# Weights and stores on GpSimd's queue, sixteen transposes by DMA, and a new instruction order in a hand-scheduled kernel

**Chip, cores, metric.** One core of one Trainium2 chip. The metric is device time in microseconds (us) of one execution.

## The reference

A decaying-state attention over 4 batches, 8 heads, 768 steps and head size 48, then a two-layer MLP with SoLU and layer norm (3072 tokens, 384 to 1024 to 384):

```python
for t in range(S):
    cur = np.einsum('bhd,bhe->bhde', u[None] * kt, vt)
    y[:, :, t] = np.einsum('bhd,bhde->bhe', rt, state + cur)
    state = wt[:, :, :, None] * state + np.einsum('bhd,bhe->bhde', kt, vt)
...
h = x @ w_in                       # x is y, rearranged to tokens x 384
e = np.exp(h - h_max); sm = e / e.sum()
solu = h * sm
ln = (solu - mean) / sqrt(var + 1e-6) * g_ln
out = ln @ w_out
```

## The kernel before

The kernel cuts time into 6 chunks of 128 steps; with 4 batches that makes 24 *units*. The whole program is one string of words. Each word is one stage of one unit, its number is the unit, and the letter behind the point is an engine, a queue or a PSUM slot. Every engine and every DMA queue carries out its words **in the order of the string**.

```python
ORDER = """
LW0.a LK0.s LU0.a LR0.s LW1.a LW2.s hot4.s3 LG0.s LK1.s lw0 LV0.a cum0.b0 LR1.s us0.s0 ex0 hot2.s3 uc0 lw1 LV1.s
p0 kp0 LW3.a LK2.a LR2.s krk0.s3 q0 krr0 cum1.b1 kr0.a hot2.s2 LV2.s ...
...                                              # 57 rows left out
o23.a out23
"""
```

The words that matter here: `LW LK LR LV` load a unit's w, k, r, v and `LI LO` the MLP's weights; `lw cum ex kp` make the scaled k and r; `krk krr kr` turn them on TensorE (PE) and copy them out of PSUM, `KD` does the same with one DMA; `y` is the attention's result, `X xT` turn it on PE and copy it, `XD` does that by DMA; `H e he hq` are the hidden layer, its exponential, their product and its square; `Oa Ob ... o out` are the output matmuls, the scaling and the store; `ce` centres the second weight matrix.

```python
    queue = {"s": sp, "a": act}
    ...
    def turned_kr(i, x):                                   # KD
        sp.dma_start_transpose(out=kr_s[i % NKP], in_=kp_t[i % NKP].rearrange("t j h d -> t (j h d)"))

    def turned_x(i, x):                                    # XD
        sp.dma_start_transpose(out=xT_t[i % NWK], in_=y_t[i % NWK])

    def hidden_mul(i, x):                                  # he: one input in PSUM
        dve.tensor_mul(out=he_t[i % NWK], in0=live[i]["h_ps"], in1=e_t[i % NWK])

    def hidden_square(i, x):                               # hq: both inputs in SBUF
        he, hq = he_t[i % NWK], hq_t[i % NWK]
        if x == "a":
            act.activation(out=hq, in_=he, func=SQUARE)
        else:
            (dve if x == "d" else pool).tensor_mul(out=hq, in0=he, in1=he)

    def store(i, x):
        c, b = units[i]
        sp.dma_start(out=out[b * S + c * C:b * S + (c + 1) * C, :], in_=o_t[i % NWK])
```

The softmax here doesn't subtract the row's maximum and nothing guards it: scores larger than these inputs give would overflow.

## Time and profile before

| | before |
|---|---|
| median of 4 runs (range) | 152.42 us (151.28 to 153.02) |
| span of the profiled run, mean granted PE clock | 151.6 us, 0.994 |
| start of the first / last o_ps matmul | 33.7 / 146.8 us |
| from there to the end | 4.8 us |

The first and the last matmul into o_ps are good milestones: before the first one the kernel loads, after the last one it only scales and stores. (The prediction had three of the four runs, with a median of 152.2.) First, the row of VectorE's (DVE's) squares in the table of instruction groups (busy us, mean ns, idle us before):

```profile
L89 DVE TENSOR_TENSOR hq<-he 128x1024 bf16<-128x1024 bf16 x11 | 8.2, 757 | 0.0
```

The median of the eleven is 681 ns, so the mean hides a longer one. The timeline (start us, length us) shows it between GpSimd's (POOL's) instructions:

```profile
86.78 1.00 POOL L89 TENSOR_TENSOR p<-kr_in 128x384 bf16<-128x384 f32 x1
87.73 1.55 POOL L89 TENSOR_SCALAR_AFFINE_SELECT m<-m 128x1024 bf16<-128x1024 bf16 x1
...
86.91 1.42 DVE L89 TENSOR_TENSOR hq<-he 128x1024 bf16<-128x1024 bf16 x1
```

The square begins while GpSimd's `p` runs and ends 0.55 us after `p` has ended, and the mask that follows takes 1.55 us in place of its usual 1.1. So it reads as if the two engines took turns: the square's real 0.68 us begins about where `p` ends, and the mask waits for it.

### The profile page before, as it was taken

Reading aid. Unit: us, or ns where it says so; the run is one execution under the profiler, and the core shown is the slowest. Engines: PE = TensorE matmul, PEld = TensorE weight load, DVE = VectorE, ACT = ScalarE, POOL = GpSimd, SP = SyncE. Lnnn points to the kernel's source line nnn. Section 1 sums busy time; section 2 is a strip of 40 time slices with the busy share of each in tenths; the row PEclk is TensorE's granted clock in tenths of the full one; section 3 lists DMA queues with packets and bytes.
Section 4 is the critical chain, followed back from the end, with each engine's and each line's share of the span. In section 5 each row is a group of like instructions: output and inputs, shape, how many; then the busy total and the mean of one; then the engine's idle time right before and its main releaser. Section 6 shows DMA issues by size and latency. Waiting matters only on the chain.

```text
span 151.6 us, 5258 instructions
## 1 busy us (share of the span) xinstructions
PE 137.2 (91%) x2156; PEld 106.6 (70%) x2158; DVE 127.9 (84%) x235; ACT 117.9 (78%) x238; POOL 94.9 (63%) x127
## 2 busy tenths in 40 slices
PE   4799787879999997999988999999999999999980
PEld 1145566467788776888777797878887888889650
DVE  5209797999999996999976999999998998688940
ACT  3465766599999997999798688999898997484442
POOL 7484993531879859993849999299847682500000
PEclk9999999999999999999999999999999999999997
DMA  5999999999983999989699999898950111011142
GB/s 110 259 257 334 405 335 255 178 210 188 224 179 121 229 217 193 215 176 241 142 243 208 230 175 232 162 230 193 248 164 6 52 56 52 4 52 56 52 160 104
DMA packets 104825, 27.08 MB, mean 179 GB/s; under 512 B 100313, under 2 KB 104418, under 8 KB 104802
## 3 DMA queue, kind: packets, MB, share of 16 engines
q1 hardware_dynamic: 94256, 24.26, 69.6%
q10 hardware_dynamic: 10546, 2.49, 7.3%
q8 instruction: 17, 0.28, 0.7%
q14 instruction: 6, 0.05, 0.1%
HBM read 22.03 MB, written 4.72 MB: 176 GB/s over the span
## 4 chain that ended last, share of the span: by engine, by line
PE 54%; DMA 12%; SPq 10%; DVE 8%; ACT 6%; POOL 4%; issue 4%; ACTq 0%; POOLq 0%
PE o_ps L89 22%; PE h_ps L89 13%; SPq L89 10%; DMA w_in<-in_w_dram 6%; PE kr_ps L89 4%; PE y_ps L89 4%; DMA kr_in<-in_r_dram 4%; PE s_ps L89 3%; PE cum_ps L89 3%; PE m_ps L89 3%; DMA v_in<-in_v_dram 3%; PE x_ps L89 2%; DVE he L89 1%; POOL m L89 1%; DVE w L89 1%
## 5 line engine op out<-in xcount | busy, mean ns | idle before, releaser
L89 PE MATMUL o_ps<-w,he 128*128 128x385 bf16 x192 | 45.7, 325 | 0.1
L89 PE MATMUL h_ps<-xT,win_sb 128*128 128x128 bf16 x576 | 35.9, 219 | 0.3 <-DVE xT L89 0.3
L89 PEld LDWEIGHTS <-win_sb 128*128 128x128 bf16 x576 | 33.0, 98 | 0.9 <-issue 0.4
L89 PE MATMUL o_ps<-inv_col,e 128*128 128x1 bf16 x192 | 31.7, 165 | 0.0
L89 DVE TENSOR_TENSOR he<-h_ps,e 128x1024 bf16<-128x1024 f32 x24 | 29.1, 1216 | 2.7 <-ACT e L89 2.5
L89 PE MATMUL o_ps<-one_col,hq 128*128 128x1 bf16 x192 | 31.3, 163 | 0.0
L89 ACT ACTIVATE e<-h_ps 128x1024 bf16<-128x1024 f32 x24 | 24.5, 1020 | 4.7 <-PE h_ps L89 4.6
L89 DVE TENSOR_TENSOR kp<-cum_ps,kr_in 128x768 bf16<-128x768 f32 x24 | 22.7, 948 | 5.9 <-ACT cum_ps L89 5.6
L89 PEld LDWEIGHTS <-hq 128*128 128x128 bf16 x192 | 18.5, 96 | 12.8
L89 POOL TENSOR_TENSOR p<-kr_in 128x384 bf16<-128x384 f32 x24 | 24.4, 1018 | 3.7 <-DMA kr_in<-in_r_dram 3.6
L89 POOL TENSOR_TENSOR dv<-vb,dg 128x384 bf16<-128x384 bf16 x24 | 19.8, 830 | 9.6 <-DVE dg L89 7.4
L89 POOL TENSOR_SCALAR_AFFINE_SELECT m<-m 128x1024 bf16<-128x1024 bf16 x15 | 16.8, 1120 | 13.4 <-ACT sq L89 5.8
L89 POOL TENSOR_TENSOR q<-p,u_bc 128x384 bf16<-128x384 bf16 x24 | 21.8, 911 | 1.9 <-ACT u_bc L89 1.7
L89 PEld LDWEIGHTS <-kp 128*128 128x128 bf16 x272 | 17.4, 98 | 6.0 <-DVE kp L89 2.1
L89 ACT ACTIVATE cum_ps<-cum_ps 128x768 f32<-128x768 f32 x24 | 19.2, 802 | 3.0 <-PE cum_ps L89 2.9
L89 PE MATMUL kr_ps<-ident,kp 128*128 128x128 bf16 x192 | 18.0, 222 | 2.3 <-ACT gr L89 0.8
L89 PEld LDWEIGHTS <-he 128*128 128x128 bf16 x192 | 18.4, 96 | 0.9
L89 PEld LDWEIGHTS <-e 128*128 128x128 bf16 x192 | 18.4, 96 | 0.5 <-issue 0.2
L89 ACT ACTIVATE lw<-w_in 128x384 bf16<-128x384 f32 x24 | 12.4, 523 | 4.1 <-DMA w_in<-in_w_dram 4.1
L89 ACT CAST m<-m_ps 128x1024 bf16<-128x1024 f32 x15 | 15.0, 1013 | 0.7 <-PE m_ps L89 0.6
L89 DVE TENSOR_TENSOR m<-m_ps,keep 128x1024 bf16<-128x1024 f32 x9 | 10.9, 1215 | 4.2 <-PE m_ps L89 4.2
L89 ACT ACTIVATE hq<-he 128x1024 bf16<-128x1024 bf16 x13 | 13.7, 1057 | 0.0
(82 smaller groups left out, 262.5 us busy)
## 6 DMA issues: line engine op xcount, KB each, us to landing
kr_in<-in_r_dram SPq DMA_DIRECT2D x24, 192.0 KB, 4.3
out_dram<-o SPq DMA_DIRECT2D x24, 192.0 KB, 3.2
kr_in<-in_k_dram SPq DMA_DIRECT2D x21, 192.0 KB, 3.5
w_in<-in_w_dram SPq DMA_DIRECT2D x21, 192.0 KB, 4.2
v_in<-in_v_dram SPq DMA_DIRECT2D x20, 192.0 KB, 4.1
wout_f<-in_moe_w_out_dram SPq DMA_DIRECT2D x2, 768.0 KB, 7.7
win_f<-in_moe_w_in_dram SPq DMA_DIRECT2D x2, 512.0 KB, 5.1
v_in<-in_v_dram ACTq DMA_DIRECT2D x4, 192.0 KB, 4.2
```

The source lines that it names most:

```text
L89: made = make(*args, **kwargs)
```

## The change

Intent: let ScalarE (ACT) issue fewer DMAs and GpSimd more, take transposes off PE where PE alone is the bound, and put more PE work ahead of the first output matmul. The diff, cut to its core (rows of the order left out; all of them differ):

```diff
-LW0.a LK0.s LU0.a LR0.s LW1.a LW2.s hot4.s3 LG0.s LK1.s lw0 LV0.a cum0.b0 LR1.s us0.s0 ex0 hot2.s3 uc0 lw1 LV1.s
+LI0.p pc0 LW0.a LU0.s LK0.a LR0.s hot8.s3 LW1.a LR1.s LW2.s lw0 LK2.s LK1.a wi0.p cum0.b0 ur0 hot3.s3 lw1 LW3.s
+ex0 p0 cum1.b1 hot5.s3 ex1 kp0 LR2.s LV0.a p1 kp1 krk0.s0 us0.s3 LW4.s krr0 uc0 kr0.d krk1.s2 lw2 q0 LV1.a LK3.s
 ...
+ex20 sel17 qm10 st17 XD15 hq13.a kp20 vb19.p Y16.ns2 LW22.s dv17 Ob11 e14 y16.d LK22.s dg18 q19 cum21.b1 lv10
+he14 S18.s3 sq11 ex21 p20 Oa12.s2 LR22.s XD16 o10.a kp21 dv18 M19.b0 Y17.ns0 qm11 Ob12 dg19 out10.p lv11 KD20
 ...
-    queue = {"s": sp, "a": act}
+    queue = {"s": sp, "a": act, "p": pool}
+    def round_u(i, x):
+        dve.tensor_copy(out=u_b, in_=u_row)
-        pe.matmul(ps["u"], lhsT=ones_row, rhs=u_row, start=True, stop=True)
+        pe.matmul(ps["u"], lhsT=ones_row, rhs=u_b, start=True, stop=True)
-        sp.dma_start(out=out[b * S + c * C:b * S + (c + 1) * C, :], in_=o_t[i % NWK])
+        queue[x or "s"].dma_start(out=out[b * S + c * C:b * S + (c + 1) * C, :], in_=o_t[i % NWK])
```

The building of constants moves unchanged into a stage behind the first weight load. Sixteen of the 24 stores and three of the five weight loads go to GpSimd; VectorE gets 14 squares instead of 11, and 4 of its 8 centrings go to GpSimd.

## The prediction

> **What bounds the kernel now.** I read four views of the profile before, in this order: the totals and the slices, the chain of work that ended last in order of time, the table of engines by stretch, and the waits. The totals and slices first:
>
> ```profile
> PE 137.2 (91%) x2156; PEld 106.6 (70%) x2158; DVE 127.9 (84%) x235; ACT 117.9 (78%) x238; POOL 94.9 (63%) x127
> PE   4799787879999997999988999999999999999980
> DMA  5999999999983999989699999898950111011142
> ```
>
> A slice is 3.8 us. TensorE is nearly always busy, and the DMA engines are full until about slice 29, which is 109 us, when the last input has been issued; then they are all but idle. So there is free DMA time only at the end. A busy TensorE is not one at its peak, so the chain has to say where it is the bound:
>
> ```profile
> 20.62 4.20 SPq L89
> 24.87 1.16 SPq L89
> 26.07 3.79 DMA w_in<-in_w_dram
> 29.88 0.37 ACTq L89
> 30.67 0.49 ACT mean_sb L89
> ...
> 91.37 2.26 DVE he L89 x2
> 93.63 0.47 DVE st L89
> 94.15 0.99 PE o_ps L89 x12
> ...
> 106.63 0.22 PE kr_ps L89 x4
> 106.86 1.34 PE h_ps L89 x24
> ...
> 109.03 0.19 PE x_ps L89 x3
> ...
> 140.38 5.98 PE o_ps L89 x84
> ```
>
> Three stretches show. Up to 33.7 us (the first o_ps) the chain goes through SyncE's queue, DMAs and an issue on ScalarE's queue: loading bounds. From 33.7 to about 94 us it changes between TensorE, ScalarE, VectorE and, at 73 to 82 us, GpSimd. From 94 to 146.4 us it is TensorE without a break. The table by stretch agrees (columns: stretch, its length, busy PE, PEld, DVE, ACT, POOL, clock, DMA share, GB/s):
>
> ```profile
> 0.00:33.70 33.70, 26.24 (x265) 15.45 (x268) 22.94 (x57) 20.54 (x37) 21.78 (x41) 1.00 1.08 262
> 33.70:72.00 38.30, 37.25 (x637) 30.14 (x637) 36.35 (x59) 36.17 (x75) 28.23 (x34) 1.00 0.94 197
> 95.00:146.40 51.40, 51.40 (x874) 42.55 (x873) 46.78 (x84) 40.45 (x86) 25.27 (x29) 1.00 0.41 102
> ```
>
> In the middle PE, VectorE and ScalarE are all within 6% of full, so no engine alone can be relieved there. In the last stretch only PE is full, at full clock. The waits show what the queues cost (engine, operation, releaser: total us, times, longest):
>
> ```profile
> ACT w L89 <- DMA v_in<-in_v_dram: 2.5, 1, 2.5
> ACT xT L89 <- DMA w_in<-in_w_dram: 1.9, 1, 1.9
> SPq L89 <- DVE o L89: 25.3, 9, 7.2
> ```
>
> Both ScalarE waits lie before 33.7 us. Neither operation reads the DMA it is put down to: ahead of each, ScalarE's queue had to issue a v load (23.51 and 29.88 us in the timeline), and that issue waited for an older DMA. The 25.3 us of SyncE waiting for o are nearly all after 109 us, where nothing is left to load; they cost little.
>
> **What the Trainium skill says.** (1) "DMA: Bandwidth & Descriptors", section "Issuing engines are not separate DMA queues": DMAs from all issuing engines run on the same 16 engines, and spreading them saves only sequencer time. The trace agrees as far as it can: in the first 33.7 us two queues together hold the DMA share at 1.08, so moving issues to GpSimd makes no bandwidth. (2) "VectorE: DVE Perf Modes", section "The three transpose paths": a 128x128 bf16 transpose takes 390 ns on TensorE and 1309 ns through the DMA crossbar. In this trace TensorE's 128x128 transpose is recorded at 219 ns and, pipelined, takes the chain some 0.06 us (four in 0.22). The crossbar is not in the trace before. (3) "DMA: Bandwidth & Descriptors", section "Latency and other measured facts": effective rate of a DMA transpose 261 GB/s in one kernel, and first byte 0.6 us from a hardware queue against about 1 us from GpSimd's. No run here shows either yet; the trace's own floor for a DMA is the o store, 1.8 us at least and 3.2 us in the median from issue to landing.
>
> **The change, part by part.**
>
> *Turning by DMA.* k and r of six units: 48 transposes leave PE, in twelve groups of four at 0.22 to 0.25 us of the chain, say 0.23: 2.8 us. y of ten units: 30 transposes, ten groups of three at 0.17 to 0.19: 1.8 us. Together 4.5 us of PE, and by the order nearly all of it after 94 us, where PE alone bounds. The copies go too: six kr copies (five on VectorE at 0.68, one on ScalarE at 1.01) and ten xT copies (three on VectorE at 0.35, seven on ScalarE at 0.48), so 4.4 us each of VectorE and ScalarE, mostly beside PE. Added: sixteen DMAs on SyncE's queue. An estimate for one, from the page's 261 GB/s and the trace's 1.8 us floor: a y (128x384 bf16, 98 KB) 0.4 + 1.8 = 2.2 us, plus 0.5 to 1 us of issue, so about 3; a kr (262 KB) 1.0 + 1.8 + 1, about 4. The order gives a kr some 9 us or more between kp and the scores, so these are hidden. The y of units 14 to 21 have some 4 to 8 us, hidden. The last two are not: between y22 ready and H22 stand the rest of H21 (about 0.9), Oa19 0.83, Y23 0.37 and Ob19 0.83, so 2.9 us; between y23 ready and H23 about H22 1.34, Oa20 0.83 and a little, 2.3 us. With 3 us and more for one, and two in a row on a queue, I count 1.5 us of new PE waiting at the end. The net of the part is -3.0 us.
>
> *The start.* Counting the order's stages with the chain's pieces (H 1.34, each half of O 0.83, kr 0.45, S 0.46, Y 0.37, cum and M 0.33, X 0.17), the PE work that stands ahead of the first Oa is 14.3 us before and 18.1 us after; all PE work is 121.5 and 117.1 (the 4.4 of the transposes again). So if Oa0 still starts at 33.7 us, 3.8 us less is left behind it. Against it: the order also puts 9.44 MB of loads and weights ahead of Oa0 instead of 8.85, and 0.59 MB at the 262 GB/s of this stretch is 2.2 us, if those loads are really in the way. For it: the two ScalarE stalls of 2.5 and 1.9 us go, since ScalarE issues only for units 0 and 1. The weights' bytes don't change, so DMA still sets the pace; of 3.8 us I count 2.5. Rounding u to bf16 makes one f32 matmul of two passes (1.6 us of PE) a single short one, and twelve more warm-up matmuls fill idle PE; both lie in the loading stretch, 0.
>
> *Stores from GpSimd.* Sixteen stores and three weights become GpSimd's to issue. At an estimated 1 us each (the page's first-byte figure; SyncE's own issue takes 0.38 us at least) that is 19 us on an engine with 95 of 152 busy. It loses four masks (1.12 each) and four v casts (0.50) and gains four centring adds. It is still below PE, but its queue is in order: a store that waits for o holds back the next bonus product or mask. I count +0.5. On the other side SyncE no longer holds a load behind an o that is late; before 109 us that was worth about nothing. The very last store is GpSimd's, with a later first byte: +0.5.
>
> *Moved work.* VectorE gives ten o scalings (0.61) to ScalarE and takes four score copies (1.22) and three squares (0.75) from it; with the copies that go, VectorE falls by some 5 us and ScalarE by some 3. That is room in the middle, counted as 0 because three engines are full there.
>
> Sum: -3.0 - 2.5 + 0.5 + 0.5 = -4.5 us. Span 151.6 gives 147.1; the median time before, 152.2, lies 0.6 over the profiled span, so about **147.5 us**, a ratio of 0.97.
>
> **The rivals.** *DMA transposes are slow.* If one takes 5 us or more, or keeps the 16 engines busy far longer than its bytes, M18 to M22 and H14 to H19 wait too, and the remaining loads, queued behind it on the same queue, come late. For it: SyncE issued loads back to back at about 0.8 us until 109 us, so that its queue has no slack when the first kr transposes start, and five of the six kr precede the last load. Against it: DMA share falls to 0.10 to 0.17 after 113 us. Two us more for each of the last y, and a few waits for kr, make it 151 to 154. *Loading becomes the bound.* The last v load stands with 22.5 us of PE work left, where it had 40.4. If DMA can't bring it by about 120 us, PE waits. By 113 us the DMA engines had moved 24.8 MB, which is about what is due ahead of that load after, plus some 1.8 MB of transposes, some 9 us at 205 GB/s: close to the limit, so 148 to 150. *The start gains all.* If Oa0 starts at 31 to 32 us with 18.1 us of PE work done, and the transposes hide, it is 151.6 - 4.5 - 3.8 - 2, about 142 to 143.
>
> **Range and chances.** The middle is 147.5; the third rival sets the lower end and the first two the upper: 143.6 to 151.0. 149.2 is the border for faster by over 2%. The PE saving stands on a chain without a break, so I give 0.68 to faster, 0.23 to within 2%, 0.09 to slower, this last all from the first rival.
>
> **What would show it.** Right: PE transposes 144 kr and 42 x in place of 192 and 72; the chain from about 90 us to the end again almost all PE; the first o_ps at 32 to 35 us; no ScalarE wait over 1 us on a load it doesn't read; y transposes landing in about 3 us; PE waiting 1 to 2 us in all before H22 and H23. Wrong: landings of 5 us or more, PE idle for kr or xT before 130 us, DMA or SyncE's queue in the chain between 90 and 125 us, the first o_ps after 36 us, or GpSimd in the chain behind a store. A late o_ps would make the start's term wrong; PE waiting for a transpose before unit 22 would make the saving of 4.5 us wrong.

## The result, and the profile after

The changed kernel took 157.35 us in the median of 4 runs (156.86 to 158.65), a ratio of 1.035, 95% interval 1.026 to 1.044: slower. (A ratio is the mean time of one kernel's fast runs over the mean of the other's fast runs of the same rounds, so not quite the ratio of the medians. Medians of before differ by chip, 152.4 to 153.8, so each experiment below is read by its ratio.) All outputs are right. The spans split at the two milestones:

| us | before | after | difference |
|---|---|---|---|
| first o_ps matmul | 33.7 | 38.5 | +4.8 |
| from first to last o_ps matmul | 113.1 | 111.4 | -1.7 |
| from there to the end | 4.8 | 6.1 | +1.3 |
| span | 151.6 | 156.0 | +4.4 |

By the prediction's count of stages, the new order leaves 99.0 us of PE work behind the first Oa in place of 107.2. The middle part should have shrunk by 8.2 us and shrank by 1.7: about **6.5 us are lost there**, on top of the late start and the longer tail. Totals, PE's slices and its granted clock of the changed kernel (a slice is 3.9 us):

```profile
PE 136.0 (87%) x2088; PEld 104.8 (67%) x2091; DVE 130.0 (83%) x220; ACT 114.6 (73%) x238; POOL 106.4 (68%) x142
PE   6658698999599999799999999999579999998950
PEclk9968999999999999999999999999978999999995
```

Against before's line in the prediction: GpSimd is busier by 11.5 us, and VectorE, with fifteen fewer instructions, is busier too. Slice 29 (counting from 1, some 109 to 113 us) has a hole in PE, and the clock is down in the two slices behind it.

**The start.** The timeline of the changed kernel, then of the one before (in brackets: idle before, and what ended it):

```profile
8.96 0.52 ACT L87 ACTIVATE lw<-w_in 128x384 bf16<-128x384 f32 x1 [4.91 <-DMA w_in<-in_w_dram]
...
10.22 1.94 DVE L87 TENSOR_TENSOR kp<-cum_ps,kr_in 128x768 bf16<-128x768 f32 x2 [6.74 <-ACT cum_ps L87]
```

```profile
6.55 0.96 DVE L89 TENSOR_TENSOR kp<-cum_ps,kr_in 128x768 bf16<-128x768 f32 x1 [3.44 <-ACT cum_ps L89]
```

The new order has `lw1` ahead of `ex0` on ScalarE. `lw1` needs the w of unit 1, which takes 7.0 us from issue to landing in place of 4.1 and is there at 8.9 us in place of 6.2, and so ScalarE stands for 4.91 us although unit 0 is ready; its first `kp` comes at 10.22 instead of 6.55 us. That 3.7 us is not made up before the first o_ps.

**The hole in PE.** The chain of work from 108 to 118 us, SyncE's own timeline (SPq) just before, and the `y` of unit 16:

```profile
108.16 5.95 DMA xT<-y
...
114.15 2.05 PE h_ps L87 x24
...
116.84 1.48 PE o_ps L87 x12
```

```profile
103.41 2.48 SPq L87 DMA_TRANSPOSE xT<-y  x1
...
107.18 0.88 SPq L87 DMA_DIRECT2D kr_in<-in_r_dram  x1
108.16 1.32 SPq L87 DMA_TRANSPOSE xT<-y  x1
```

```profile
104.99 0.56 DVE L87 TENSOR_TENSOR y<-y_ps,dv 128x384 bf16<-128x384 f32 x1
```

The y of unit 16 was ready at 105.5 us. Its transpose was issued at 108.16, behind the transpose of unit 15, which held the queue for 2.48 us, and three loads; it landed at 114.1. From y to xT that is 8.6 us: 2.6 us in the queue, and then 5.95 us from the start of its issue to its landing, with those three loads just ahead of it and a kr transpose (5.4 us to land) just behind. The other y transposes whose landing the profile tells took 2.3 to 3.7 us. PE waited 2.9 us of the 8.6:

```profile
PE h_ps L87 <- DMA xT<-y: 3.7, 2, 2.9
```

And the wait was paid again: the two groups behind it took 2.05 and 1.48 us, where the same groups take 1.34 and 0.83 at full clock. By the table of stretches of 2 us the granted clock was 0.74, 0.50 and 0.91 from 114 to 120 us; one minus the clock times PE's busy time there is 1.7 us. One late transpose cost PE **2.9 + 1.7 = 4.6 us** in this stretch.

**GpSimd and VectorE.** Groups of the changed kernel:

```profile
L87 DVE TENSOR_TENSOR hq<-he 128x1024 bf16<-128x1024 bf16 x14 | 15.4, 1098 | 0.1
L87 POOL DMA_DIRECT2D out_dram<-o x16 | 9.2, 574 | 18.7 <-ACT o L87 7.9 <-DVE o L87 6.0 <-ACT lv L87 3.6
```

A store takes 0.57 us of GpSimd, but GpSimd also stands idle for 18.7 us ahead of the stores, most of it until an o is scaled (7.9 us on ScalarE, 6.0 on VectorE). And a square on VectorE takes 1098 ns in the mean instead of 757, with a longest one of 3.02 us. At the median of before (681 ns) fourteen would take 9.5 us, not 15.4.

### The profile page after: what moved, and what is told of

Same layout as the page of the kernel before. It is cut to its first block, busy times and chain, and to the rows that moved or that the text cites. A ratio compares the mean times of both kernels' runs of the same rounds, so it can differ in the third digit from the quotient of the medians.

```text
span 156.0 us, 5157 instructions
## 1 busy us (share of the span) xinstructions
PE 136.0 (87%) x2088; PEld 104.8 (67%) x2091; DVE 130.0 (83%) x220; ACT 114.6 (73%) x238; POOL 106.4 (68%) x142
## 4 chain that ended last, share of the span: by engine, by line
DVE 33%; PE 29%; issue 12%; ACT 8%; DMA 7%; SPq 6%; POOL 1%; POOLq 0%; DVEq 0%; ACTq 0%
PE o_ps L87 12%; DVE kp L87 7%; PE h_ps L87 7%; SPq L87 6%; DVE he L87 6%; ACT cum_ps L87 4%; DMA xT<-y 4%; DVE st L87 4%; DVE hq L87 3%; DMA kr_in<-in_k_dram 3%; PE y_ps L87 3%; DVE w L87 3%; DVE dg L87 3%; DVE m L87 3%; DVE y L87 2%
## 5 line engine op out<-in xcount | busy, mean ns | idle before, releaser
L87 PE MATMUL o_ps<-w,he 128*128 128x385 bf16 x192 | 46.3, 328 | 0.1
L87 PE MATMUL h_ps<-xT,win_sb 128*128 128x128 bf16 x576 | 36.5, 221 | 4.0 <-DMA xT<-y 3.7
L87 PEld LDWEIGHTS <-win_sb 128*128 128x128 bf16 x576 | 33.6, 99 | 5.6 <-DMA xT<-y 3.8
L87 PEld LDWEIGHTS <-hq 128*128 128x128 bf16 x192 | 18.7, 97 | 13.4 <-issue 0.7
L87 POOL TENSOR_TENSOR dv<-vb,dg 128x384 bf16<-128x384 bf16 x24 | 20.3, 847 | 9.9 <-ACT rs L87 3.6
L87 POOL DMA_DIRECT2D out_dram<-o x16 | 9.2, 574 | 18.7 <-ACT o L87 7.9
L87 POOL TENSOR_SCALAR_AFFINE_SELECT m<-m 128x1024 bf16<-128x1024 bf16 x11 | 13.1, 1192 | 8.3 <-ACT m L87 8.3
L87 PEld LDWEIGHTS <-kp 128*128 128x128 bf16 x224 | 14.4, 98 | 5.5 <-DVE st L87 1.6
L87 DVE TENSOR_TENSOR m<-m_ps,keep 128x1024 bf16<-128x1024 f32 x13 | 15.8, 1217 | 1.9 <-PE m_ps L87 1.9
L87 DVE TENSOR_TENSOR hq<-he 128x1024 bf16<-128x1024 bf16 x14 | 15.4, 1098 | 0.1
L87 PE MATMUL kr_ps<-ident,kp 128*128 128x128 bf16 x144 | 13.4, 221 | 1.9 <-DVE st L87 1.5
```

The costliest lines, as they stand in the source:

```text
L87: made = make(*args, **kwargs)
```

## The experiments

Theory at first: the lateness of the transposes, the start, and the stores each add their share. Rivals: the new order in itself is worse, or the transposes are innocent and only the stores hurt. The kernels named `b_` start from the kernel before and take over one part; those named `a_` start from the changed kernel and undo one.

### Stores from GpSimd, on the old order: `b_stores_pool` and `b_stores_sq`

`b_stores_pool` issues the same 16 stores from GpSimd, each where it stood:

```diff
-    queue = {"s": sp, "a": act}
+    queue = {"s": sp, "a": act, "p": pool}
-... out0 sel6 o1.a lw9 M7.b0 out1 ...
+... out0.p sel6 o1.a lw9 M7.b0 out1.p ...      (also 2-4, 6-8, 10, 14, 16-20, 23)
```

> The kernel before, with the same 16 stores as in the change issued from GpSimd instead of SyncE, each where it stood in the order. Theory (stores on GpSimd cost about 1%: GpSimd waits for o, its work is pushed together and shuts VectorE out): ratio 1.005 to 1.02, GpSimd waiting for o 10 to 20 us, VectorE's squares longer than their 757 ns mean. Rival (the cost seen in the new order is that order's own): ratio 0.995 to 1.005, squares unchanged.

Measured: 157.69 us, ratio 1.034 (1.027 to 1.042). **This one part alone costs as much as the whole change.** It is also more than the theory allowed (1.02). First o_ps at 33.9, last at 149.9, end at 156.0: against before +0.2 us up to the first, +2.9 between the two and +1.3 in the tail. The group of squares, the square of unit 9, and GpSimd's timeline around it:

```profile
L89 DVE TENSOR_TENSOR hq<-he 128x1024 bf16<-128x1024 bf16 x11 | 13.3, 1218 | 0.0
```

```profile
87.41 3.93 DVE L89 TENSOR_TENSOR hq<-he 128x1024 bf16<-128x1024 bf16 x1
...
88.22 1.08 POOL L89 TENSOR_SCALAR_AFFINE_SELECT m<-m 128x1024 bf16<-128x1024 bf16 x1
89.26 0.49 POOL L89 CAST vb<-v_in 128x384 bf16<-128x384 f32 x1
89.71 1.08 POOL L89 TENSOR_SCALAR_AFFINE_SELECT m<-m 128x1024 bf16<-128x1024 bf16 x1
94.22 0.58 POOL L89 DMA_DIRECT2D out_dram<-o  x1 [3.42 <-DVE o L89]
```

Compare with the same square in before, which was let in after one GpSimd instruction. Here it stands beside `p` and the three instructions shown, and ends at 91.34, 0.55 us after the run ends (90.79) and GpSimd falls idle to wait for an o. The square of unit 3 took 3.12 us instead of 0.78 in a similar way (it got in between two `p`). The squares have the same data and number as before; the operation `he`, with one input in PSUM, took 1216 ns in the mean in both kernels. GpSimd ran the same words without a gap around unit 9 in before too, so a busy GpSimd alone doesn't decide who is let in; why the square lost its turn here is not shown.

The delay appears at this place: the h_ps matmuls of unit 12 start 0.5 us later than in before (89.66 and 89.16 us), those of unit 13 3.0 us later (99.06 and 96.04), and those of unit 20 still 3.0.

The Trainium skill has the mechanism: "SBUF — State Buffer", section "Who interferes with whom", says that "A DVE instruction with two SBUF inputs contends with a GpSimd instruction that reads SBUF" and that the pair of ports is an exclusive lock. The trace agrees, except that the wait spans several instructions of the other engine. Whether the two waits are the cause is tested by giving just these two squares to ScalarE, with the stores left on GpSimd:

```diff
-hq3.d ... hq9.d
+hq3.a ... hq9.a
```

> The kernel before with the 16 stores from GpSimd, and in addition the squares of units 3 and 9 (the two that took 3.12 and 3.93 us on VectorE) given to ScalarE. Theory (VectorE being shut out of SBUF by GpSimd's back-to-back work is what costs): 3.0 of the 4.4 us come back less what ScalarE loses, ratio 1.01 to 1.02, VectorE's squares all below 1.5 us. Rival (the stores cost in another way, GpSimd's lateness itself): ratio 1.03 or more still, other groups late.

Measured: 153.48 us, ratio 1.003 (1.001 to 1.005). The squares of VectorE are at their own length again:

```profile
L89 DVE TENSOR_TENSOR hq<-he 128x1024 bf16<-128x1024 bf16 x9 | 6.3, 706 | 0.0
```

More came back than either theory expected: the last o_ps matmul starts at 145.4 us, 4.5 us earlier than in `b_stores_pool` and 1.4 earlier than in before. What is left of the stores' cost is the tail, 6.2 us instead of 4.8. The place where the delay appears and this test together make the locked-out squares, that of unit 9 above all, the cause of the 2.9 us in the middle. The test alone would not: it also takes two squares off VectorE, which may be worth something in itself, as the 1.4 us against before suggest, and the control (before with only these two squares on ScalarE) was not run.

### Transposes, on the old order: `b_turns`, `b_kd`, `b_xd`, `b_turns_last`, `b_turns_free`

`b_turns` takes over both kinds, each DMA issued right behind what it reads; `b_kd` only k and r of units 18 to 23, `b_xd` only y of units 14 to 23:

```diff
-kp18 ... krk18.s2 ... krr18 ... kr18.d     (b_turns, b_kd: units 18-23)
+kp18 KD18
-y16.d ... X16.s2 ... xT16.a                (b_turns, b_xd: units 14-23)
+y16.d XD16
```

> The kernel before with the same sixteen transposes done by DMA (y of units 14 to 23 just behind the y, k and r of 18 to 23 just behind kp, all from SyncE) and nothing else changed. Theory (the DMA transposes in themselves are about neutral: 4.5 us of PE work gained, waits for xT of 1 to 3 us each for some units lost, the start and the middle are as before): first output matmul at 33 to 34 us, time 150.5 to 154. Rival A (the transposes are what made the change slower): 155 or more. Rival B (they gain what was predicted and all the loss is elsewhere): 148 to 150.

> The kernel before with only k and r of units 18 to 23 turned by DMA, y all on TensorE. Theory (what b_turns lost are the xT waits of 3 to 4 us each on the path, while kr has slack between kp and the scores): PE work falls by 2.8 us and nothing waits: 149.5 to 152 where before is about 152.5. Rival (SyncE's 1.3 us of issue per transpose delays loads and stores, or the masks and squares take longer): 153 to 156.

> The kernel before, with only y of units 14 to 23 turned by DMA, each issued right behind its y (30 PE transposes and ten copies less). Theory (the path from y to xT grows from about 1 us to 4 us or more, PE waits for it): slower than before by 1 to 3%, PE waits for xT of 2 to 4 us in all, the loads of units 21 to 23 up to 2 us late. Rival (only the k and r transposes hurt): within 1% of before, or faster by up to 1.8 us, the PE time saved.

Measured: `b_turns` 158.68 us, ratio 1.032 (1.020 to 1.044); `b_kd` 157.65 us, 1.029 (1.018 to 1.039), its profiled run slow; `b_xd` 152.51 us, 0.997 (0.995 to 1.000), its profiled run slow as well, the ratio from 17 fast ones. So `b_turns` lies in the range of its Rival A, `b_kd` missed its theory (149.5 to 152) and `b_xd` fits its rival. **The y transposes by themselves are hidden**; with k and r among the last loads they aren't. In `b_turns`, SyncE's queue, the chain and the table by stretch (columns as in the prediction, the clock third from last):

```profile
101.52 1.96 SPq L87 DMA_TRANSPOSE kr<-kp  x1
...
106.73 1.31 SPq L87 DMA_TRANSPOSE kr<-kp  x1
...
108.76 1.98 SPq L87 DMA_DIRECT2D v_in<-in_v_dram  x1
110.86 1.44 SPq L87 DMA_TRANSPOSE xT<-y  x1
```

```profile
110.86 2.95 DMA xT<-y
...
113.85 2.74 PE h_ps L87 x24
```

```profile
112.00:114.00 2.00, 0.15 (x2) 0.15 (x3) 0.46 (x1) 0.81 (x3) 2.00 (x4) 0.75 0.83 166
114.00:116.00 2.00, 2.00 (x21) 2.00 (x20) 0.00 (x0) 0.00 (x0) 0.49 (x1) 0.50 1.20 241
116.00:118.00 2.00, 2.00 (x20) 1.29 (x18) 0.32 (x1) 1.09 (x2) 0.00 (x0) 0.50 0.92 221
```

Here the queue is the larger part: the y of unit 16 was ready at 101.9 us, its transpose was issued 8.9 us later, behind two kr transposes, five loads and a store, and landed 2.95 us after that. PE does nearly nothing from 112 to 114 us (it waited 2.76 us for the xT), and then runs at half clock to about 120 us: the group of 24 matmuls took 2.74 us instead of 1.34. Reckoned as above, pause and clock cost 2.8 + 3.0 us, more than the 4.4 us of PE work that all sixteen transposes save. The h_ps matmuls of unit 15 start 1.2 us earlier than in before, those of unit 16 1.3 us later and those of unit 17 4.1 us later: the loss arises here, and it is the 4.1 us by which the span is longer. `b_kd` shows the same once, with a kr: PE waited 2.6 us for it at 118 us, and the clock was 0.50 to 0.53 from 120 to 126. That profile is of a slow run, so I lean on `b_turns` for the mechanism and on `b_kd` for the ratio of its fast runs. In `b_xd` PE's longest wait for an xT was 0.3 us, and every slice of the clock but the last is full:

```profile
PEclk9999999999999999999999999999999999999996
```

SyncE's queue is late in both: a transpose takes 1.2 to 2.6 us to issue where most plain loads take 0.4 to 0.9, and the last v load is issued at 108.3 us in before, 114.2 in `b_xd` and 116.0 in `b_turns`. The xT of unit 16 even lands at the same time, 113.9 us in `b_xd` and 113.8 in `b_turns`. But PE, with the k and r transposes still to do (and in a slow run that was already 1.0 us behind before's at unit 15), came to it only at 113.6 us in `b_xd`, and at 111.1 in `b_turns`; only the long pause was followed by half clock. So "hidden" was a near thing in `b_xd`.

Two more kernels put transposes only behind the last load: y of units 17 to 23, k and r of 22 and 23. The second also moves stores 11 to 23 to GpSimd, so that none that waits for its o stands ahead of a transpose:

```diff
+y17.d XD17 ... kp22 KD22 ... kp23 KD23                       (b_turns_last, b_turns_free)
+out11.p ... out23.p                                          (b_turns_free)
```

> The kernel before, with y of units 17 to 23 and k, r of 22 and 23 turned by DMA: all of these stand behind the last load on SyncE's queue, so no load is held up and the DMA engines are idle but for stores. PE is spared 21 + 16 transposes, about 2.2 us. Theory A (the queue shared with the loads is the cause): span 149 to 151, ratio 0.985 to 1.0. Theory B (the transpose's own 4 to 5 us is the cause, PE waits in any case): ratio 1.0 to 1.03, PE waits for xT or kr of 2 us or more, and the clock dips after them.

> As b_turns_last, with stores 11 to 23 from GpSimd, so that no store that waits for its o stands ahead of a transpose on SyncE's queue. Theory A (queue): better than b_turns_last by 1 to 2 us, 148 to 150. Theory B (own time): equal to b_turns_last within 1%, the waits stay. The last store from GpSimd lands later by about 1 us in either.

Measured: 152.40 us, 0.998 (0.994 to 1.002), and 154.12 us, 1.009 (1.005 to 1.013). Behind the last load the transposes cost nothing that the times show, though one of k and r still takes 4.7 us in the median to land (of two; PE waited 0.9 us for one, in a slow profile). That speaks for the place, among the last loads, and not for the transpose's own time; but these are also fewer transposes, and without the units at which `b_turns` and `b_kd` waited. The theory of the shared queue holds in that. It also said that freeing the queue of stores would gain 1 to 2 us; instead the kernel lost 1.1%, and its tail is that of a kernel with GpSimd's stores (last o_ps 145.7, end 151.4). And the PE time saved, 2.2 us by the prediction's rates, became 0.2% of 152: the saving is hardly to be had on the old order either.

### The start and the loads: `a_start`, `b_loads_sp`

```diff
-LI0.p pc0 LW0.a ... wi0.p cum0.b0 ... lw1 LW3.s ex0 ... p1 ... wi1.p     (a_start)
+pc0 LW0.a ... cum0.b0 ex0 ... lw1 LW3.s ... p1 LI0.p ... wi0.p wi1.p
-LV4.a ... LV5.a                                                          (b_loads_sp)
+LV4.s ... LV5.s
```

> The changed kernel with two words of its start moved: the exponential of unit 0 stands again ahead of the logarithm of unit 1 on ScalarE, and the first weight load (with its cast) is issued after unit 1's first bonus product instead of first of all. Theory (the start lost 4.8 us because the first weight load delays the loads of units 0 and 1, and because ScalarE sits 4.9 us in front of unit 1's logarithm with unit 0's exponential behind it): kp of unit 0 at 6.5 to 7.5 us instead of 10.2, the first output matmul at 35 us or earlier instead of 38.5, time 153 to 155. Rival (the start makes no difference because the stretch up to 64 us is bound by VectorE and the DMA engines anyway): first output matmul at 37.5 or later, time 156.5 to 158.

> The kernel before with the v loads of units 4 and 5 issued from SyncE instead of ScalarE: the two issues ahead of which ScalarE stood for 2.5 and 1.9 us. Theory of the prediction (they hold up the start): the two waits go, first output matmul 0.5 to 2 us earlier than 33.7, time 150.5 to 152. Rival (SyncE's queue is full there, so v of 4 and 5 come later and VectorE or ScalarE wait for them): no gain, 152 to 154.

`a_start`: 156.15 us, 1.027 (1.018 to 1.035), against 1.035. `kp0` at 6.4 us, as expected; the first o_ps at 36.4 in place of 38.5, not at 35, and the time lies between theory and rival. Moving the exponential and the first weight load with its cast explains about 2 of the 4.8 us at most (kernels with the start of the changed one had the first o_ps at 37.3 to 38.5), and the rest stays. `b_loads_sp` takes away the two stalls of ScalarE that the prediction counted as a gain: 1.001 (0.998 to 1.005). In its profile the first o_ps does come 2.5 us earlier, at 31.2 us (a run at full clock up to there); at the first o_ps of unit 2 0.5 us of that are left (43.3 against 43.8). **In this kernel an earlier first o_ps was worth nothing at the end**, so the milestone at the start must not be added to the others without a test.

### Undoing parts in the new order: `a_stores_sp`, `a_start_stores`, `a_xd_early`, `a_combined`

```diff
-out0.p ... out23.p                       (a_stores_sp, a_start_stores, a_combined)
+out0 ... out23
-y16.d ... LK22.s ... LR22.s XD16         (a_xd_early, a_combined: each XD right behind its y)
+y16.d XD16 LK22.s ... LR22.s
                                          (a_start_stores, a_combined: also as a_start)
```

> The changed kernel with all stores issued from SyncE. Theory (GpSimd's stores cost it 25 us of issue and waiting but GpSimd is seldom on the path, so only the last store matters): 156 to 157.5. Rival (GpSimd held back behind late stores delays the bonus products and masks): 153 to 155. A third way (SyncE's queue, now with stores that wait for o between the loads and the transposes, gets later): over 158.

> The changed kernel with the start of a_start and all stores from SyncE as in a_stores_sp, each of which gave about 1.2 to 1.5 us alone. Theory (the two are independent: one is the first 36 us, the other the middle and the end): 153.5 to 155. Rival (both take away the same VectorE or GpSimd wait): 155 to 156.5.

> The changed kernel with each y transpose issued directly behind its y in SyncE's order; in effect units 16, 17 and 19 pass ahead of one or two loads. Theory (unit 16's xT came 8.6 us after its y because its transpose stood behind three loads and the transposes of another unit in one queue, PE waited 2.9 us for it and then ran at a lower clock): the wait falls under 1.5 us, no slice of the clock under 8 tenths near 112 us, time 154.5 to 156.5. Rival (the transpose itself is slow with the DMA engines full): wait still 2.5 us or more, time 156.5 to 158.

> The changed kernel with the three edits that each gained: the start of a_start, all stores from SyncE, y transposes directly behind their y. Theory (independent): ratio to before 0.995 to 1.01, first output matmul near 36.3, PE waits for xT under 2.5 us. Rival (with the stores on SyncE's queue the transposes stand behind stores that wait for o): ratio 1.01 to 1.03, waits for xT 3 us and more.

| | median us | ratio to before (95%) | first / last o_ps, end |
|---|---|---|---|
| `a_stores_sp` | 155.55 | 1.025 (1.015 to 1.034) | 38.2 / 149.5, 155.1 |
| `a_start_stores` | 155.61 | 1.012 (1.001 to 1.023) | profile slow |
| `a_xd_early` | 157.38 | 1.016 (1.002 to 1.031) | 37.3 / 147.5, 153.7 |
| `a_combined` | 156.75 | 1.023 (1.012 to 1.034) | 36.8 / 148.6, 154.3 |

By the middles of the ratios each repair helps a little against 1.035, but only the interval of `a_start_stores` lies clear of the changed kernel's (1.026 to 1.044). In `a_stores_sp` the squares fall from 15.4 to 11.4 us, the longest to 1.35. In `a_xd_early` the longest wait for an xT falls from 2.9 to 1.0 us, the clock near 112 us stays full, and the last o_ps comes 2.4 us earlier; 1.2 of that are there at the first o_ps, which this edit doesn't touch. But the parts **do not add**: all three together are no better than one. The intervals are about a per cent wide on either side, so the four can't be ranked among each other; what is shown is that none reaches the time before.

### Turning on PE again in the new order: `a_turns_pe`, `a_turns_late`, `a_kd_back`

```diff
-KD18 ... XD14
+krk18.s0 krr18 ... kr18.d ... X14.s0 xT14.a     (PSUM slots given out anew from there)
```

`a_turns_pe` puts all 16 right behind their inputs, `a_turns_late` half-way to their use; `a_kd_back` takes `a_combined` and puts only k and r back, half-way.

> The changed kernel with all sixteen DMA transposes put back on TensorE, with their copies. Theory (the transposes gave 4.5 us of PE work and cost about as much in waits for xT and in a lower clock after the wait): no PE wait for xT over 0.5 us, PE busy by some 4 us more, time 156 to 158, equal to the changed kernel within 1 us. Rival (the DMA transposes are what made it slower): time 152 to 153.5.

> A second try at undoing the transposes in the changed kernel: all sixteen back on TensorE, but with each group half way between its input and its use in TensorE's order, and its copy three stages later, instead of straight behind its input as in a_turns_pe, whose PE and VectorE stood still behind it. Theory (the first try was slow through its own placing; the transposes in the changed order are about neutral): 155 to 159, against some 157 for the changed kernel. Rival A (the DMA transposes make the change slower): 152 to 154.5. Rival B (the order needs the DMA transposes, PE and VectorE have no room for the work): over 161.

> The new order with the start mended, all stores from SyncE and each y transpose issued right behind its y (as in the combined kernel, 1.023), and now k and r of units 18 to 23 turned on TensorE again, each half-way between its kp and its scores, the copy six words behind. Theory (the k and r transposes by DMA, ahead of and among the last loads on SyncE's queue, are the rest of the loss in the new order): ratio 0.995 to 1.01. Rival (the new order is slower for other reasons, or has no place for them): 1.02 or more, PE or VectorE standing still for kr.

Measured: 168.82 us (1.110), 165.37 us (1.081) and 159.90 us (1.041, 1.032 to 1.050). None is a clean undo: the new order has no place in PE's sequence and no PSUM slot kept for the transposes, so PE and VectorE stand for each other. In `a_turns_pe` PE waited 4.2 us in one group of o_ps for a kr copy, which stood right behind a square of VectorE that took 5.07 us beside five GpSimd instructions in a row. So what the DMA transposes cost inside the new order is not settled. One run of `a_kd_back`, the profiled one, took 686 us with every PE group about three times as long; its three other runs took 158.7 to 160.0, and I leave it out. Such a run came once more, 312 us in one of the 20 runs of `b_loads_sp`; the cause is not known, and both count as slow.

### Two that settled little: `a_ce_dve`, `a_hq_act`

```diff
-ce7.p ... ce5.p ... ce0.p ... ce2.p     (a_ce_dve)
+ce7.d ... ce5.d ... ce0.d ... ce2.d
-hq5.d ... hq7.d ... hq10.d ... hq14.d   (a_hq_act)
+hq5.a ... hq7.a ... hq10.a ... hq14.a
```

> The changed kernel with all eight centring adds on VectorE, as before. Theory (VectorE and GpSimd working on bf16 tiles in SBUF at the same time slow each other: VectorE's adds were 0.83 us instead of 0.38 and GpSimd's 1.0): the eight adds take about 2.8 us in all, GpSimd is free 3.9 us earlier, the first output matmul at 36.5 to 37.5 us instead of 38.5, time 155.5 to 157. Rival (nothing, because VectorE is the bound there and gets four adds more): first output matmul at 38 to 39, time 157 to 158.

> The changed kernel with four of its VectorE squares (units 5, 7, 10, 14; recorded at 2.15, 1.40, 1.46 and 3.02 us instead of 0.68) given back to ScalarE at about 1.06 us each. Theory (VectorE's squares, with two inputs in SBUF, wait while GpSimd works through its queue without a gap, and VectorE is on the path): VectorE's squares fall from 15.4 us to about 7.5, time 155 to 156.5. Rival (these waits lie in the shadow of something else, such as the wait for unit 16's xT): 156.9 to 158.

`a_ce_dve`: 157.65 us, 1.032 (1.020 to 1.043), no gain; the first o_ps came at 41.3 us, later than either theory. `a_hq_act`: 157.90 us, 1.024 (1.011 to 1.038); the ten squares left on VectorE still took 1049 ns in the mean. In the new order moving some squares seems only to have moved the wait to others (the profile is of a slow run), unlike in `b_stores_sq`, where two squares held all of it.

## Why the prediction was wrong, step by step

- **The bound of before.** Right as far as it went: before 33.7 us loading, in the middle three engines near full, then PE. But "busy" was taken for "working". VectorE's squares contain waiting for GpSimd, and the reader of the totals can't see that; the spread between a group's median and longest instruction shows it.
- **Turning by DMA, "-3.0 us".** The PE time left as said (144 and 42 transposes), and in the median a single transpose was as said: 3.0 us for a y and 3.2 for a kr from the start of the issue to landing (1.2 to 2.5 us of it issue), against "about 3" and "about 4". The step that failed is "The y of units 14 to 21 have some 4 to 8 us, hidden". It counted one undisturbed transpose from the moment of its input. Among the last loads the y of unit 16 first waited for its turn on SyncE's in-order queue and then landed late: 2.6 + 5.95 us in the changed kernel, 8.9 + 2.95 us in `b_turns`. The prediction also had no term for the clock, which made a 2.9 us pause cost 4.6. Of "these are hidden" for kr, the changed kernel shows no PE wait for one; in `b_kd` it failed, by 2.6 us. The 1.5 us of waiting counted for the end came to 0.7 us. Two signs named for being wrong came true: PE idle for xT before 130 us (at 111 us), and landings of 5 us or more (5.95 us, and 5.4 for a kr). The first rival named the right queue, but had the loads waiting behind the transposes, where the transposes waited behind the loads; it lacked the clock.
- **The start, "-2.5 us".** "If Oa0 still starts at 33.7 us" was false: 38.5, and the named sign (after 36) came true. I counted stages and bytes and did not follow ScalarE's own order, where `lw1` stands ahead of `ex0`. The gain from the two ScalarE stalls is real at the first o_ps (2.5 us in `b_loads_sp`) and gone by the end: the step that failed there is to count time won before the first o_ps as time won at the end. About half of the delay has no single cause that I found.
- **Stores, "+0.5" and "+0.5".** The mechanism was named, a store that waits holds back the next GpSimd work. The size was off: +2.9 in the middle and +1.3 in the tail when done alone. The step that failed is the victim: with the stores there, GpSimd shut VectorE's two-SBUF squares out for 3 to 4 us, which no term of the prediction has. That it does so because a store pushes its work together is not shown. The estimated 1 us per store, taken from a first-byte figure, was 0.57 us of issue; it wasn't the busy time that cost.
- **Moved work, "0".** Not tested apart. Three more squares on VectorE in a kernel that lets GpSimd lock them out points the wrong way, but `a_hq_act` does not prove it.
- **The sum.** Alone on the old order the stores cost 4.4 us of span and the transposes 4.1, and the late start is there besides; yet the whole change costs 4.4. The new order may give part of it back, as the 8.2 us less of PE work behind the first Oa would suggest, or the losses may overlap; no run tells the two apart. How much each part costs inside the new order stays open, since its repairs do not add up.

No version beat the kernel before by more than the noise; the best is `b_xd` at 0.997. Not tried: the squares of units 3 and 9 on ScalarE with all stores left on SyncE. By the milestones of `b_stores_sq` (last o_ps at 145.4) and the tail of before (4.8) that would be 150.2 us, an estimate.

## What to carry to other kernels

Count a DMA that replaces compute from the place where it stands in its queue, behind everything issued earlier there and together with the transfers around it, and ask what a pause of 2 to 3 us in TensorE does to the clock behind it. Before giving GpSimd anything that waits, look which VectorE instructions read two SBUF operands beside it, and compare the longest of a group with its median: a lockout looks like busy time. A part that is worth a gain in one order is not worth the same in another, so test a part on the kernel that is known to be good.

## What the Trainium skill lacked or had wrong

- "SBUF — State Buffer", section "Who interferes with whom": the blocking between VectorE and GpSimd is as it says, but it speaks of one instruction. The runs show a square of 0.68 us held out over four GpSimd instructions in a row (3.93 us) and five (5.07 us), both ending only when GpSimd paused; in before one was let in after one instruction (1.42 us). The first of these squares started at 87.41 us, ahead of three of the four that it waited for (from 88.22 us on); what decides the next turn the runs don't settle.
- "TensorE: Matmul & The Clock Gate", section "What's actually happening": it gives an idle window of about 3.4 us for the fall to half clock. Here pauses of 2.6, 2.8 and 2.9 us were enough, with 0.50 granted afterwards and 3 to 7 us until it was full again; so was one of 1.85 us in `a_start` (at 112 us). A pause of 1.54 us at 41 us was followed by half clock in `a_stores_sp` and not in the changed kernel, so these runs give no fixed length.
- "VectorE: DVE Perf Modes", section "The three transpose paths": 1309 ns for a 128x128 block by DMA. Here three blocks (98 KB) landed in 2.4 to 4.1 us and eight (262 KB) in 3.2 to 4.9 us from the start of the issue, medians by kernel, and one of three blocks in 5.95 us among the last loads. Of this the issue holds the queue for 1.2 to 2.9 us; no page gives an issue time measured on this chip.
- "DMA: Bandwidth & Descriptors", section "Latency and other measured facts": it gives about 0.4 us more to the first byte from GpSimd's queue. The last store took 3.7 us from issue to the end of the span in the changed kernel, 2.8 us from SyncE in before. For the time that a store's issue holds GpSimd, 0.57 us here, the section has no figure.
